# Where the weights of the last phase are converted: w_in and w_out2 in the attention through HBM, w1 and w2 at an even pace

## The chip, the cores and the metric

The kernel runs on one core of one Trainium2 chip. The metric is the device time of one execution in microseconds (us); lower is better. A core has TensorE (PE: matmuls; its weight loads are PEld), VectorE (DVE), ScalarE (ACT), GpSimd (POOL) and SyncE (SP), whose queue issues all DMA transfers of this kernel.

## What is computed

Causal attention with a bias for 4 batches of 8 heads, 576 positions, head size 64; then two blocks of dense layers on the 2304 tokens. All arithmetic is float32.

```python
scores = q @ k.T / 8 + min(-(cum_q - cum_k), 0), causal    # cum: running sum of max(s, 0)
x = softmax(scores) @ v                                    # 2304 x 512
g = (x @ w1) * (x @ w2)                                    # 2304 x 1024
x = g @ w3 @ w_out                                         # w3: 1024 x 1024, w_out: 1024 x 512
h = x @ w_in                                               # 2304 x 1024
so = h * softmax(h)
out = (so - mean) / sqrt(var + 1e-6) * g_ln @ w_out2       # 2304 x 512
```

The weight matrices w1, w2, w3, w_out, w_in and w_out2 arrive as float64 and are handed to the kernel as their bits, two 32-bit words an element.

## The kernel before

**Splitting.** The dense matmuls run on float32r operands. Each operand is split in two: `hi` copies it to float32r on ScalarE (line 92), `lo` subtracts that copy from it (line 97, VectorE or GpSimd). A product is three matmuls: hi·hi, hi·lo, lo·hi.

**Converting weights.** A block of 128 x 512 weights (512 KB of float64 bits) is loaded by `stage`. `to_f32` puts a float32 together from the two words with one scaling on ScalarE (line 374) and three VectorE instructions (380 a shift, 381 and 384 with two inputs each). `split_w` then writes hi and lo of it. `jobs` is a list of blocks in order; `pump(n)` converts the next n and loads ahead into the `stage` buffers (2 in the attention, 4 later). For w_out2 (`wo2_conv`) a further ScalarE instruction (line 783) scales the rows by g_ln.

**Phases.** (1) Attention, a list of 36 `steps`: step st does the scores and softmax of head st (st < 8) or st - 2 (st from 10 on), the transposes of the head two earlier, the product with v every second step (`av_parts`), and `NF[st]` units of the products a = x @ w1 and b = x @ w2 for batches that are done (`ab_unit`: 24 matmuls of 288 columns; the result g goes to `g_scr` in HBM). From step 10 on, GpSimd does two subtractions a head (line 97, QA and KB). The first score tile of a step goes to a PSUM pool that from step 11 on has one buffer. `PUMP[st]` blocks of w1 and w2 (16 in all, `wab_job`) are converted in step st. (2) The last units of a and b, with 14 blocks of w_out and w3 converted between them (`AP3`). (3) The M stage: eight `m_unit`s of 24 matmuls compute M = w3 @ w_out, in split form `MH`, `ML`; after each, `pump(AM[f])` converts three blocks: the rest of w3, then the eight of w_in (`IH`, `IL`). w3's hi and lo have five buffers. (4) Last phase: chunks of 256 tokens, x2 = g @ M (`x2_unit`: four groups of 24 matmuls a chunk); for each of 18 token tiles of 128 `h_unit` (24 matmuls of 512 columns, then maximum, exponential, product, square, power, scaling over VectorE, ScalarE and GpSimd), `tr2` (8 transposes) and `out_unit` (24 matmuls of 512 columns). w_out2's eight blocks (`OH`, `OL`) are converted after x2 of chunk 0 (4) and after the first two h tiles (2 and 2).

**Order.** A planner orders the instructions of each engine by a timeline of its own; they need not stand in source order. Instructions on one engine then run in that order, and the SP queue issues transfers in its order too. `behind` keeps a conversion of the attention behind the step's first softmax tile.

Of the kernel before, what the change touches and what calls it, by code (L numbers as in the profile page):

```python
# [8 lines left out]
F32 = mybir.dt.float32  # L9
F32R = mybir.dt.float32r  # L10
U32 = mybir.dt.uint32
AF = mybir.ActivationFunctionType
ALU = mybir.AluOpType
# [6 lines left out]
CW = 512  # L20
# [5 lines left out]
def tile_attention_moe(  # L26
# [15 lines left out]
    nc = tc.nc  # L42
    B, H, D, _, S = qkT.shape
    NH = B * H
    T, DM = out.shape
    w1, w2, w3L, wo1, w_in, wo2 = (w.bitcast(U32) for w in (w1, w2, w3L, wo1, w_in, wo2))
    DF = w_in.shape[1] // 2
    KC = DM // 128
    KF = DF // 128
# [13 lines left out]
    dram = ctx.enter_context(tc.tile_pool(name="dram", bufs=1, space=DRAM))  # L63
# [4 lines left out]
    ]  # L68
    const = ctx.enter_context(tc.tile_pool(name="const", bufs=1, side="left"))

    g_scr = [dram.tile([KF, 128, S], F32, name=f"g_scr{n}") for n in range(B)]
    cum_scr = dram.tile([NH, 2, S], F32R, name="cum_scr")
    cumf_scr = dram.tile([NH, S], F32, name="cumf_scr")
# [3 lines left out]
    gln = const.tile([128, KF], F32, name="gln")  # L77
# [9 lines left out]
    def flat(ap):  # L87
        return ap.rearrange("p a b -> p (a b)")

    def hi(dst, src, eng=None):  # L90
        if eng is None:
            nc.scalar.activation(out=dst, in_=src, func=AF.Copy)  # L92
        else:
            eng.tensor_copy(out=dst, in_=src)

    def lo(dst, src, hi_, eng=nc.vector):
        eng.tensor_tensor(out=dst, in0=src, in1=hi_.bitcast(F32), op=ALU.subtract)  # L97
# [3 lines left out]
    at = attn_ctx.enter_context(tc.tile_pool(name="at", bufs=1, side="left"))  # L101
# [51 lines left out]
    V, G = nc.vector, nc.gpsimd  # L153
# [213 lines left out]
    wab = [[r0.tile([128, KC, DF // 2], F32R, name=f"W{i}{j}") for j in range(4)] for i in range(2)]  # L367
    xT = [[r0.tile([128, KC, S], F32R, name=f"xT{j}{i}") for i in "hl"] for j in range(2)]

    def to_f32(raw, eng=nc.gpsimd):  # L370

        low, high = raw[:, :, 0], raw[:, :, 1]
        if eng is None:
            nc.scalar.activation(out=high.bitcast(F32), in_=high.bitcast(F32), func=AF.Copy, scale=2.0 ** -112)  # L374
        else:
            eng.tensor_scalar(
                out=high.bitcast(F32), in0=high.bitcast(F32), scalar1=2.0 ** -112, scalar2=1.0,
                op0=ALU.mult, op1=ALU.mult,
            )
        nc.vector.tensor_scalar(out=low, in0=low, scalar1=29, scalar2=None, op0=ALU.logical_shift_right)  # L380
        nc.vector.scalar_tensor_tensor(  # L381
            out=low, in0=high, scalar=3, in1=low, op0=ALU.logical_shift_left, op1=ALU.bitwise_or,
        )
        nc.vector.scalar_tensor_tensor(
            out=low, in0=high, scalar=0x80000000, in1=low, op0=ALU.bitwise_and, op1=ALU.bitwise_or,
        )
        return low.bitcast(F32)

    def split_w(dst_h, dst_l, raw, e1=nc.gpsimd, e2=nc.gpsimd):
        t = to_f32(raw, e1)  # L390
        if len(dst_h.shape) == 3:
            t = t.rearrange("p (c f) -> p c f", c=dst_h.shape[1])
        hi(dst_h, t)
        lo(dst_l, t, dst_h, e2)

    V, G = nc.vector, nc.gpsimd
    ME = [(None, V)]
    MAT = ()
    WO2 = (0, 4, 2, 2)
    XMS = ((0, 1, 2, 3),)  # L400
    EX = 0
    AP3, AM = (2, 2, 2, 2, 2, 2, 1, 1), (3, 3, 3, 3, 3, 3, 3, 3)
    mjobs = []
    jobs = []
    loaded = []

    stg = [at, 2]

    def stage(src):
        raw = stg[0].tile([128, CW, 2], U32, tag="stage", bufs=stg[1], name="stage")  # L410
        dst = flat(raw)
        if len(src.shape) == 3:
            dst = dst.rearrange("p (c f) -> p c f", c=src.shape[1])
        if after[0] is None:
            nc.sync.dma_start(out=dst, in_=src)
        else:
            with tc.issue_after(after[0].ins):
                nc.sync.dma_start(out=dst, in_=src)
        return raw

    def load_jobs():
        while jobs and len(loaded) < stg[1]:
            src, conv = jobs.pop(0)
            loaded.append((stage(src), conv))

    def pump(n):
        for _ in range(n):
            load_jobs()
            if loaded:
                raw, conv = loaded.pop(0)  # L430

                with ExitStack() as order:
                    for ins in behind:
                        order.enter_context(tc.issue_after(ins))
                    conv(raw)
        load_jobs()

    def w_job(src, dst, eng=None):
        e1, e2 = (nc.gpsimd, eng) if eng else ME[len(mjobs) % len(ME)]
        if not eng:  # L440
            mjobs.append(0)
        jobs.append((src, lambda raw: split_w(*dst(), raw, e1, e2)))

    def wab_job(f, w):
        fs = slice((f % 4) * 128, (f % 4) * 128 + 128)
        dst = lambda: (wab[f // 4][2 * w][:, :, fs], wab[f // 4][2 * w + 1][:, :, fs])
        jobs.append(((w1, w2)[w][f], lambda raw: split_w(*dst(), raw, None, V)))

# [34 lines left out]
    for i in range(NQ, 2):  # L485
# [4 lines left out]
        out=wmask[:, S - 128:S], in_=wmask[:, S - 128:S], pattern=[[-1, 128]],  # L490
# [14 lines left out]
    for f in range(KF):  # L505
        for w in range(2):
            wab_job(f, w)


    units = [(n, i, x) for n in range(B) for i in range(KF) for x in range(2)]  # L510
# [2 lines left out]
    steps += [(h if h < NH else None, h - 2 if h >= H + 2 else None) for h in range(H, NH + 2)]  # L513
    NF = {10: 3, 11: 0, 12: 3, 13: 0, 14: 3, 15: 2, 16: 2, 17: 0, 18: 1, 19: 1, 20: 1, 21: 2, 22: 2, 23: 2, 24: 2, 25: 2, 26: 2, 27: 2, 28: 2, 29: 2, 30: 2, 31: 2, 32: 2, 33: 2, 34: 3, 35: 3}
    PD, FS = 10, 0.5
    PUMP = {3: 1, 5: 1, 6: 1, 10: 2, 11: 1, 12: 2, 13: 1, 14: 3, 15: 2, 16: 1, 17: 1}
    fill = []
    late = []
    for st, (h, ph) in enumerate(steps):
# [18 lines left out]
        if st > 1:  # L538
            pump(PUMP.get(st, 0))
        if h is not None:  # L540
# [36 lines left out]
    pm = ctx.enter_context(tc.tile_pool(name="pm", bufs=1, side="left"))  # L577
    MH = pm.tile([128, KF, DM], F32R, name="MH")
    ML = pm.tile([128, KF, DM], F32R, name="ML")
    stg[:] = pm, 4  # L580
    mctx = ExitStack()
    mp = mctx.enter_context(tc.tile_pool(name="mp", bufs=1, side="left"))
    WOH = mp.tile([128, KF, DM], F32R, name="WOH")
    WOL = mp.tile([128, KF, DM], F32R, name="WOL")
    m_st = {}
# [8 lines left out]
    def m_unit(f):  # L594
        ps = smalltile("m")
        for k in range(KF):
            H3, L3 = m_st[f, k // 4]
            for w_, o_ in ((H3, WOH), (H3, WOL), (L3, WOH)):
                nc.tensor.matmul(
                    ps, w_[:, k % 4], o_[:, k],  # L600
                    start=(k == 0 and w_ is H3 and o_ is WOH), stop=(k == KF - 1 and w_ is L3),
                )
# [3 lines left out]
    for k in range(KF):  # L606
        w_job(wo1[k * 128:k * 128 + 128], lambda k=k: (WOH[:, k], WOL[:, k]))
    for f in range(KF):
# [19 lines left out]
    r2 = ctx.enter_context(tc.tile_pool(name="r2", bufs=1, side="right"))  # L628
    IH = r2.tile([128, KC, DF], F32R, name="IH")
    IL = r2.tile([128, KC, DF], F32R, name="IL")  # L630
# [122 lines left out]

    load_g(0)
    load_g(1)
    win = []
    for i in range(8):
        c, o = divmod(i, 2)
        fs = slice(o * 512, o * 512 + 512)
        w_job(  # L760
            w_in[c * 128:c * 128 + 128, o * 1024:o * 1024 + 1024],
            lambda c=c, fs=fs: (IH[:, c, fs], IL[:, c, fs]),
        )
    for f in range(nm[0], KF):
        m_unit(f)
        pump(AM[f] if f < KF - 1 else len(jobs) + len(loaded))
        if f == 4:
            split_g(0, 0)
        if f == 5:
            split_g(0, 1)  # L770
    mctx.close()
    p2 = ctx.enter_context(tc.tile_pool(name="p2", bufs=1, side="left"))
    OH = p2.tile([128, KF, DM], F32R, name="OH")
    OL = p2.tile([128, KF, DM], F32R, name="OL")
    raws = {}

    def wo2_load(k):
        if k < KF:
            raws[k] = stage(wo2[k * 128:k * 128 + 128])

    def wo2_conv(k):
        t = to_f32(raws.pop(k), None)
        nc.scalar.activation(out=t, in_=t, func=AF.Copy, scale=gln[:, k:k + 1])
        hi(OH[:, k], t)
        lo(OL[:, k], t, OH[:, k])
        wo2_load(k + 4)

    nwo = [0]

    def wo2_pump(c):  # L790
        for _ in range(c):
            wo2_conv(nwo[0])
            nwo[0] += 1

    for k in range(4):
        wo2_load(k)
    wo2_pump(WO2[0])
    for i, ms in enumerate(XMS):
        x2_unit(0, *ms)
        wo2_pump(WO2[1 + i])  # L800
    split_g(1, 0)
    split_g(1, 1)
    load_g(2)
# [3 lines left out]
    for t in range(NT + 2):  # L807
        c, o = divmod(t, 2)
        if t < NT:
            h_unit(t)  # L810
        if t < NT and c + 1 < NCH and 2 * t >= EX:
            x2_unit(c + 1, 2 * o)
        if 0 <= t - 1 < NT - 1:
            tr2(t - 1)
        if t < NT and c + 1 < NCH and 2 * t + 1 >= EX:
            x2_unit(c + 1, 2 * o + 1)
        if t < 2:
            wo2_pump(WO2[2 + t])
        if 0 <= t - 2 < NT:
            out_unit(t - 2)  # L820
        if t == NT:
            tr2(t - 1)
        if t < NT and c + 2 < NCH:
            split_g(c + 2, o)
            if o == 1 and c + 3 < NCH:
                load_g(c + 3)
# [50 lines left out]
```

## Time and profile before

| | us |
|---|---|
| median of 3 runs (lowest, highest) | 779.66 (778.08, 780.28) |
| the profiled execution | 779.51 |
| its span, first to last instruction | 777.7 |
| TensorE busy, mean granted clock | 749.4, 0.989 |
| VectorE, ScalarE, GpSimd busy | 466.0, 412.9, 97.3 |

The span is cut into stages by what TensorE does: attention with a and b up to about 349 us, the rest of a and b to 400, M to 444.6, then the last phase. Matmuls are pipelined, and a matmul's own length in a row is longer than its share: 24 x matmuls in a row take 2.81 us, 0.117 each, though one is listed at some 0.29. So "busy" says only that TensorE had something under way; how dense it was is read from the number of matmuls in a stage. The clock is the granted one; 1.00 is 2.4 GHz, and the other level is half of it. A wait "<-X" names what ended an engine's idle time.

### The profile page before, as it was taken

The page shows a single profiled execution, that of the slowest core. Times are in us where ns is not written, and L with a number is a line of the kernel's source. Part 1 is how long each engine was busy: PE and PEld are TensorE (multiplying, and loading weights), DVE is VectorE, ACT ScalarE, POOL GpSimd, SP SyncE. Part 2 cuts the span into 40 slices and gives each one's busy share as a digit, 9 for nine tenths or more (in the row PEclk, how much of TensorE's full clock was granted, in tenths as well). Part 3 has the DMA queues.
Part 4 walks back from the last instruction along what each step waited for, and adds up shares of the span by engine and source line. Part 5 has one row for each costly group of instructions (what it writes and reads, how often), then busy time and mean ns, then how long its engine had stood idle before and what let it go on. Part 6 is the DMA issues. An engine that isn't in the chain of part 4 may idle for free.

```text
span 777.7 us, 13025 instructions
## 1 busy us (share of the span) xinstructions
PE 749.4 (96%) x4864; PEld 653.1 (84%) x4864; DVE 466.0 (60%) x1186; ACT 412.9 (53%) x951; POOL 97.3 (13%) x117
## 2 busy tenths in 40 slices
PE   8989997999999999999999997999999999999997
PEld 5657876888888988899988886888888888888885
DVE  5897989986556564327958889642424353432241
ACT  4987876898766666425536567532323342322232
POOL 6022322233223221000000000000000000000000
PEclk9999998999999999999999999999999999999999
DMA  5543544434332321017659554102112000000001
GB/s 136 173 120 97 170 144 145 145 97 136 109 93 81 106 76 34 31 47 246 214 182 340 169 190 135 55 14 68 47 50 69 14 14 13 15 14 14 14 28 41
DMA packets 38039, 75.59 MB, mean 97 GB/s; under 512 B 6796, under 2 KB 18060, under 8 KB 37976
## 3 DMA queue, kind: packets, MB, share of 16 engines
q1 hardware_dynamic: 37976, 74.76, 31.5%
q8 instruction: 38, 0.62, 0.3%
q14 instruction: 25, 0.20, 0.1%
HBM read 60.36 MB, written 14.38 MB: 96 GB/s over the span
## 4 chain that ended last, share of the span: by engine, by line
PE 80%; DVE 8%; DMA 7%; issue 2%; ACT 1%; POOL 1%; SPq 0%; DVEq 0%; ACTq 0%; POOLq 0%
PE o L746 13%; PE a L338 12%; PE b L338 12%; PE h L697 11%; PE x L677 11%; PE av L310 5%; PE tr L277 4%; PE sc L182 3%; PE sc L190 2%; PE sc L191 2%; PE tr L735 2%; DMA stage<-in_w_dram 2%; DMA stage<-in_w_in_dram 2%; DMA graw<-g_scr 1%; DVE stage L381 1%
## 5 line engine op out<-in xcount | busy, mean ns | idle before, releaser
L208 ACT ACTIVATE P<-P,STAT 64x64 f32<-64x64 f32 (+4 forms) x160 | 88.0, 551 | 32.0 <-DVE STAT L204 29.4
L705 DVE TENSOR_REDUCE sv<-h 128x1 f32<-128x1024 f32 x18 | 22.0, 1225 | 114.6 <-PE h L697 114.6
L677 PE MATMUL x<-gh,MH 128*128 128x256 f32 x288 | 82.9, 288 | 0.0
L677 PE MATMUL x<-gh,ML 128*128 128x256 f32 x288 | 81.5, 283 | 0.0
L677 PE MATMUL x<-gl,MH 128*128 128x256 f32 x288 | 81.5, 283 | 0.0
L204 DVE CUSTOM_DVE_ANT_0 P<-sc,wmask 64x64 f32<-64x64 f32 (+4 forms) x160 | 70.9, 481 | 13.0 <-PE sc L182 8.7
L719 POOL TENSOR_TENSOR sv<-sv,mhalf 128x1 f32<-128x1 f32 x18 | 9.9, 551 | 455.8 <-DVE sv L716 455.8
L97 POOL TENSOR_TENSOR QA<-qk,QB 64x576 fp32r<-64x576 f32 x24 | 35.6, 1482 | 206.8 <-ACT QB L92 168.4
L338 PE MATMUL b<-xT0h,W 128*128 128x288 f32 x256 | 58.1, 301 | 3.3 <-ACT W L92 2.2
L697 PE MATMUL h<-IH,x2h 128*128 128x512 f32 x144 | 56.6, 393 | 3.4 <-ACT x2h L92 1.9
L338 PE MATMUL a<-xT0h,W 128*128 128x288 f32 x256 | 58.7, 303 | 0.0
L697 PE MATMUL h<-IH,x2l 128*128 128x512 f32 x144 | 57.0, 396 | 1.5 <-DVE x2l L97 1.5
L746 PE MATMUL o<-OH,lh 128*128 128x512 f32 x144 | 57.1, 397 | 0.3 <-ACT lh L92 0.3
L338 PE MATMUL a<-xT1h,W 128*128 128x288 f32 x256 | 57.1, 298 | 0.0
L746 PE MATMUL o<-OH,ll 128*128 128x512 f32 x144 | 57.0, 396 | 0.0
L746 PE MATMUL o<-OL,lh 128*128 128x512 f32 x144 | 56.8, 395 | 0.0
L697 PE MATMUL h<-IL,x2h 128*128 128x512 f32 x144 | 56.5, 393 | 0.0
L338 PE MATMUL b<-xT1h,W 128*128 128x288 f32 x256 | 56.5, 294 | 0.0
L677 PEld LDWEIGHTS x<-gh,MH 128*128 128x128 f32 x288 | 55.5, 193 | 0.7
L677 PEld LDWEIGHTS x<-gl,MH 128*128 128x128 f32 x288 | 55.3, 192 | 0.8
L374 ACT ACTIVATE stage<-stage 128x512 f32<-128x512 f32 x56 | 38.3, 689 | 32.5 <-DMA stage<-in_w_dram 13.3
L677 PEld LDWEIGHTS x<-gh,ML 128*128 128x128 f32 x288 | 55.2, 192 | 0.1
(121 smaller groups left out, 1921.2 us busy)
## 6 DMA issues: line engine op xcount, KB each, us to landing
stage<-in_w_dram SPq DMA_DIRECT2D x32, 512.0 KB
qk<-in_qk_dram SPq DMA_DIRECT2D x48, 288.0 KB
g_scr<-g_sb SPq DMA_DIRECT2D x32, 288.0 KB
stage<-in_wo_dram SPq DMA_DIRECT2D x16, 512.0 KB
graw<-g_scr SPq DMA_DIRECT2D x6, 1024.0 KB
out_dram<-o SPq DMA_DIRECT2D x18, 256.0 KB
VT<-in_vm_dram SPq DMA_DIRECT2D x16, 256.0 KB
stage<-in_w_in_dram SPq DMA_DIRECT2D x8, 512.0 KB
```

The costliest lines, as they stand in the source:

```text
L97: eng.tensor_tensor(out=dst, in0=src, in1=hi_.bitcast(F32), op=ALU.subtract)
L182: nc.tensor.matmul(view, QN[h % 2][:, q0:q0 + rows], KN[h % 2][:, c0:c0 + view.shape[-1]], start=True, stop=True,)
L204: mx = nc.vector.tensor_tensor_reduce(out=dst2, in0=ps_in, in1=msk, scale=-SCALE, scalar=BIG, op0=ALU.add, op1=ALU.min, accum_out=st[0:row ...
L208: ex = nc.scalar.activation(out=dst, in_=dst, func=AF.Exp, bias=st[0:rows, ti:ti + 1], scale=-1.0, accum_out=st[0:rows, 5 + ti:6 + ti],)
L277: nc.tensor.transpose(ps[:, c:c + 128], pt[:, QOF[i] + 128 * j:QOF[i] + 128 * j + 128], ident)
L310: nc.tensor.matmul(st["ps"][64 * e:64 * e + 64, 448 + c0:448 + c1], vr[:, j, e], PT[(2 * p + e) % 4][:, o + c0:o + c1], **kw,)
L338: nc.tensor.matmul(ps, w_[:, c, fs], x_[:, c, sl], start=(c == 0 and w_ is WH and x_ is XH), stop=(c == KC - 1 and w_ is WL),)
L374: nc.scalar.activation(out=high.bitcast(F32), in_=high.bitcast(F32), func=AF.Copy, scale=2.0 ** -112)
L677: nc.tensor.matmul(ps[m], w_[:, k, m * 128:m * 128 + 128], g_[:, k], start=(k == 0 and w_ is MH and g_ is GH), stop=(k == KF - 1 and w_ is ...
L697: nc.tensor.matmul(ps[:, hf], x_[:, k, ts_], w_[:, k, hf * 512:hf * 512 + 512], start=(k == 0 and x_ is XH and w_ is IH), stop=(k == KC - ...
L705: nc.vector.reduce_max(out=sv[:, 0:1], in_=psf, axis=AX.X, negate=True)
L746: nc.tensor.matmul(ps, l_[:, k], w_[:, k], start=(k == 0 and l_ is LH and w_ is OH), stop=(k == KF - 1 and l_ is LL),)
```

## The change

- w_in's and w_out2's 16 blocks become jobs behind those of w1 and w2. In the attention each is loaded, converted to float32 into a new tile `cst` (two buffers), for w_out2 scaled by g_ln, and stored to `wf_scr` in HBM (256 KB).
- `PUMP`: w1 and w2 go two a step in steps 10 to 15 and one in step 16; the 16 new jobs one a step in steps 18 to 33.
- In the M stage `pump(AM[f])` converts two blocks, of w3 alone. The stored blocks are read back into four `wf` buffers; after each `m_unit` one block of w_in is split into hi and lo. w_out2's blocks are split four and four after the first two h tiles; none is split before.
- The `stage` buffers of the later phases lie in the pool that ends with the M stage.

```diff
+    wf_scr = [dram.tile([128, CW], F32, name=f"wf_scr{i}") for i in range(16)]
...
-    def to_f32(raw, eng=nc.gpsimd):
+    def to_f32(raw, eng=nc.gpsimd, dst=None):
...
+        res = low if dst is None else dst.bitcast(U32)
         nc.vector.scalar_tensor_tensor(
-            out=low, in0=high, scalar=0x80000000, in1=low, op0=ALU.bitwise_and, op1=ALU.bitwise_or,
+            out=res, in0=high, scalar=0x80000000, in1=low, op0=ALU.bitwise_and, op1=ALU.bitwise_or,
         )
-        return low.bitcast(F32)
+        return res.bitcast(F32)
...
-    WO2 = (0, 4, 2, 2)
...
-    AP3, AM = (2, 2, 2, 2, 2, 2, 1, 1), (3, 3, 3, 3, 3, 3, 3, 3)
+    AP3, AM = (2, 2, 2, 2, 2, 2, 1, 1), (2, 2, 2, 2, 2, 0, 0, 0)
...
+    def spill_job(i):
+        src = w_in[i // 2 * 128:i // 2 * 128 + 128, i % 2 * 1024:i % 2 * 1024 + 1024] if i < 8 else wo2[(i - 8) * 128:(i - 7) * 128]
+
+        def conv(raw):
+            t = at.tile([128, CW], F32, tag="cst", bufs=2, name="cst")
+            to_f32(raw, None, t)
+            if i >= 8:
+                nc.scalar.activation(out=t, in_=t, func=AF.Copy, scale=gln[:, i - 8:i - 7])
+            nc.sync.dma_start(out=wf_scr[i], in_=t)
+
+        jobs.append((src, conv))
...
+    for i in range(16):
+        spill_job(i)
...
-    PUMP = {3: 1, 5: 1, 6: 1, 10: 2, 11: 1, 12: 2, 13: 1, 14: 3, 15: 2, 16: 1, 17: 1}
+    PUMP = {3: 1, 5: 1, 6: 1, 10: 2, 11: 2, 12: 2, 13: 2, 14: 2, 15: 2, 16: 1, 18: 1, 19: 1, 20: 1, 21: 1, 22: 1, 23: 1, 24: 1, 25: 1, 26: 1, 27: 1, 28: 1, 29: 1, 30: 1, 31: 1, 32: 1, 33: 1}
...
-    stg[:] = pm, 4
...
+    stg[:] = mp, 4
...
+    def wf_load(i):
+        if i < 16:
+            wf[i] = r2.tile([128, CW], F32, tag="wf", bufs=4, name="wf")
+            nc.sync.dma_start(out=wf[i], in_=wf_scr[i])
+
+    def wf_split(i, eng):
+        t = wf.pop(i)
...
+        hi(h_, t)
+        lo(l_, t, h_, eng)
+        wf_load(i + 4)
+
+    for i in range(4):
+        wf_load(i)
     for f in range(nm[0], KF):
         m_unit(f)
-        pump(AM[f] if f < KF - 1 else len(jobs) + len(loaded))
+        pump(AM[f])
+        wf_split(f, V)
...
     for i, ms in enumerate(XMS):
         x2_unit(0, *ms)
-        wo2_pump(WO2[1 + i])
...
         if t < 2:
-            wo2_pump(WO2[2 + t])
+            for k in range(4):
+                wf_split(8 + 4 * t + k, V)
```

## Rows read from the trace of the kernel before

**Rows 1.** busy tenths of 40 equal slices of the span (the page)

```profile
PE   8989997999999999999999997999999999999997
```

**Rows 2.** stages: length, busy us of each engine (instructions), granted clock, DMA share, GB/s

```profile
80.00:140.00 60.00, 50.91 (x361) 46.67 (x360) 54.19 (x144) 46.03 (x114) 17.41 (x11) 0.94 0.48 145
140.00:180.00 40.00, 40.00 (x321) 33.84 (x319) 35.96 (x116) 35.70 (x102) 14.68 (x10) 1.00 0.45 126
200.00:320.00 120.00, 120.00 (x947) 109.28 (x946) 69.96 (x239) 79.61 (x216) 26.15 (x18) 1.00 0.26 77
400.90:444.60 43.70, 43.68 (x193) 36.15 (x194) 33.33 (x60) 23.80 (x40) 0.00 (x0) 1.00 0.76 249
444.60:488.50 43.90, 36.60 (x235) 33.13 (x234) 39.55 (x77) 29.91 (x53) 0.56 (x1) 0.95 0.49 155
```

**Rows 3.** TensorE in order of time, 457 to 488: start, length, [idle before <-releaser]

```profile
459.62 0.50 PE L697 MATMUL h<-IH,x2h 128*128 128x512 f32 x1 [1.92 <-ACT x2h L92]
480.62 0.47 PE L697 MATMUL h<-IH,x2h 128*128 128x512 f32 x1 [1.50 <-DVE so L711]
484.19 0.50 PE L697 MATMUL h<-IH,x2l 128*128 128x512 f32 x1 [1.49 <-DVE x2l L97]
487.08 1.25 PE L735 MATMUL tr<-ident,so 128*128 128x128 f32 x7 [2.39 <-DVE so L720]
```

**Rows 4.** matmuls of line 677 (x), then of line 697 (h), in one stage

```profile
444.60:488.50 43.90, 22.06 (x169) 21.72 (x169) 0.95 0.49 155
...
444.60:488.50 43.90, 14.93 (x57) 10.70 (x57) 0.95 0.49 155
```

**Rows 5.** chain that ended last, a full stretch: start, length, what

```profile
508.09 5.49 PE h L697 x24
...
548.81 2.81 PE x L677 x24
551.62 0.87 PE tr L735 x8
```

**Rows 6.** conversions, 444.6 to 488.5: form, count | busy us, mean ns | idle before

```profile
L381 DVE SCALAR_TENSOR_TENSOR stage<-stage 128x512 uint32<-128x512 uint32 x13 | 8.9, 686 | 0.0
...
L374 ACT ACTIVATE stage<-stage 128x512 f32<-128x512 f32 x12 | 8.3, 694 | 6.2 <-DMA stage<-in_w_in_dram 3.8 <-DMA stage<-in_wo_dram 2.4
...
L783 ACT ACTIVATE stage<-stage,gln 128x512 f32<-128x512 f32 x8 | 6.0, 762 | 1.7 <-DVE stage L384 1.6
...
L380 DVE TENSOR_SCALAR stage<-stage 128x512 uint32<-128x512 uint32 x12 | 5.1, 425 | 1.9 <-DMA stage<-in_wo_dram 1.2 <-DMA stage<-in_w_in_dram 0.4
```

**Rows 7.** VectorE, first softmax tile of heads 16 and 31 (16 such rows)

```profile
156.27 0.74 DVE L204 CUSTOM_DVE_ANT_0 P<-sc,wmask 128x576 f32<-128x576 f32 x1
...
313.47 0.75 DVE L204 CUSTOM_DVE_ANT_0 P<-sc,wmask 128x576 f32<-128x576 f32 x1
```

**Rows 8.** conversions, 80 to 140: count | busy us, mean ns | idle before

```profile
L380 DVE TENSOR_SCALAR stage<-stage 128x512 uint32<-128x512 uint32 x8 | 7.7, 977 | 1.4 <-DMA stage<-in_w_dram 1.4
...
L97 DVE TENSOR_TENSOR W<-stage,W 128x512 fp32r<-128x512 f32 x8 | 6.2, 782 | 0.0
```

**Rows 9.** GpSimd and VectorE in order of time, 115 to 121

```profile
115.47 1.73 POOL L97 TENSOR_TENSOR QA<-qk,QB 64x576 fp32r<-64x576 f32 x1 [12.91 <-ACT QB L92]
...
115.82 1.67 DVE L380 TENSOR_SCALAR stage<-stage 128x512 uint32<-128x512 uint32 x1
...
120.91 0.74 DVE L204 CUSTOM_DVE_ANT_0 P<-sc,wmask 128x576 f32<-128x576 f32 x1
```

**Rows 10.** TensorE's waits, 80 to 140: total us, times, longest

```profile
PE sc L190 <- issue: 3.8, 1, 3.8
PE b L338 <- ACT W L92: 2.2, 2, 1.1
PE sc L190 <- DVE g_sb L358: 1.9, 1, 1.9
PE b L338 <- DVE g_sb L358: 1.1, 1, 1.1
```

More of the change, by code (lines that the diff above doesn't have):

```diff
@@ L755, in tile_attention_moe @@
     load_g(1)
[L756 to L763, printed above, removed]
+    wf = {}
+    def wf_load(i):
[4 more added lines that the diff above has]
+        t = wf.pop(i)
+        if i < 8:
+            c, fs = i // 2, slice(i % 2 * 512, i % 2 * 512 + 512)
+            h_, l_ = IH[:, c, fs], IL[:, c, fs]
+        else:
+            h_, l_ = OH[:, i - 8], OL[:, i - 8]
+        hi(h_, t)
[3 more added lines that the diff above has]
+        wf_load(i)
     for f in range(nm[0], KF):
         m_unit(f)
-        pump(AM[f] if f < KF - 1 else len(jobs) + len(loaded))
+        pump(AM[f])
+        wf_split(f, V)
         if f == 4:
@@ L774, in tile_attention_moe @@
     OL = p2.tile([128, KF, DM], F32R, name="OL")
[L775 to L797, printed above, removed]
     for i, ms in enumerate(XMS):
         x2_unit(0, *ms)
-        wo2_pump(WO2[1 + i])
     split_g(1, 0)
```

## The prediction

> **What bounds the kernel now.** I read the 40 slices first, then the busy times of single stages, then the waits in the stages where TensorE is not full. TensorE is full in nearly every slice [rows 1], and its matmuls are the same before and after the change. So the change can only take away time in which TensorE stands still or runs at its lower clock, or add such time. Two stretches before the last phase have it and are touched by the change [rows 2]: 80 to 140 us (50.91 us busy of 60, so 9.09 us idle, granted clock 0.94) and 444.6 to 488.5 us (36.60 of 43.9, so 7.30 us idle, clock 0.95). Between them, from 140 to 180, from 200 to 320 and through the M stage (400.9 to 444.6), TensorE is busy throughout. There VectorE and ScalarE may be given work as long as TensorE never waits for them.
>
> In the later stretch TensorE starts x2 and h. Four waits make up the 7.30 us [rows 3]: 1.92 for x2h on ScalarE, 1.50 and 1.49 for VectorE's `so` and x2l, 2.39 for the normalised `so` that the first transposes need. None of these is a conversion of a weight, but each stands in its engine's queue among such conversions: VectorE is busy 39.55 of 43.9 us here [rows 2]. How long would the stretch be without stalls? It holds 169 x matmuls and 57 h matmuls [rows 4], and the 8 transposes of one token tile. Where TensorE is full, 24 x take 2.81 us, 24 h take 5.49, 8 transposes 0.87 [rows 5]. 169 x 2.81/24 = 19.8, 57 x 5.49/24 = 13.0, and 0.9 and one last M matmul (0.2) give 33.9. So 43.9 - 33.9 = 10.0 us are lost: 7.3 idle, some 2.2 to the lower clock (0.05 x 43.9), the rest in small pieces.
>
> **Part 1: w_in and w_out2 leave the M stage and the start of the last phase.** Each of the 16 blocks costs here VectorE 0.43 + 0.69 and a second 0.69 (line 384 runs the same form as line 381), that is 1.81 us, and ScalarE 0.69, and 0.76 more for each of the 8 w_out2 blocks [rows 6]. For 16 blocks that is 29 us of VectorE and 17.1 us of ScalarE, from the second half of the M stage to 488 us. The hi and lo of each block stay, fed from 256 KB instead of 512 KB. In the late stretch VectorE ran 12 or 13 of each of the three ops, ScalarE 12 and 8 [rows 6]: about 12.5 x 1.81 = 22.6 of 39.55 us and 14.4 of 29.91 us go. VectorE falls to under half of the stretch, and x2h, x2l and `so` no longer queue behind three or four conversions. What is late next is the chain of the first h tile (maximum, exponential, product, square, power, scaling) up to its transposes; TensorE has x2 of chunk 1 (4 units of 24 at 2.81, 11.2 us) and the second h tile (5.49) to cover it, which is what it has in each later tile, where it is full [rows 5]. I take it that 2.0 us stay, about the largest of the four waits [rows 3], so 8.0 of 10.0 are won. The ends: 10.0, and 5.0 if two of the four waits stay with their share of the clock.
>
> The M stage loses w_in's conversions and keeps two w3 blocks a step. VectorE's 33.33 of 43.70 us falls, and TensorE already is full there: no gain. A loss is possible, since four reads of the spilled blocks (1 MB) stand on SP ahead of the w3 loads, with transfers at 249 GB/s in this stage [rows 2]: 1 MB is 4.2 us. The w3 tiles are held back by their five buffers anyway, so I put this at nothing, and at 4 us if that cover is gone. What lies behind 488 us is full and untouched; its first o needs the w_out2 splits, which now stand behind a 256 KB read instead of a 512 KB load and four ops.
>
> **Part 2: sixteen conversions in the attention, steps 18 to 33.** By the first softmax tile of their heads these steps run from 156 to about 314 us, 16 steps [rows 7]. Each adds three VectorE ops, one or two ScalarE ops, a 512 KB load and a 256 KB store. From 200 to 320 us, 11 of the 16 steps begin, and VectorE is busy 69.96 of 120 us, ScalarE 79.61, TensorE 120.00 [rows 2]. With GpSimd's subtractions beside them the ops stretch: in 80 to 140 us line 380 took 0.98 on average instead of 0.43 [rows 6, 8], which makes 0.98 + 2 x 0.69 = 2.36 us of VectorE a block. 11 x 2.36 = 26 and ScalarE 11 x 0.69 + 8 x 0.76 = 14 bring both to 94 to 96 of 120 us. For 140 to 180 the row shows VectorE at 35.96 and ScalarE at 35.70 of 40, with conversions of w1 and w2 among it, and TensorE at 40.00. So that load is known to be hidden, and I cost the sixteen at 0. What hides them are the two a/b units a step; steps 18 to 20 have one only. The other end is the stretch at 80 to 140: 9.09 us idle and 0.06 x 60 = 3.6 us of clock over 8 conversions [rows 2, 8] is 1.59 us each. A spilled block lacks the lo of 0.78 [rows 8]: 2.36 of 3.14 us on VectorE, so 1.59 x 0.75 x 16 = 19 us. The load and the store add 80 GB/s to the 77 of that stretch; 249 GB/s is carried elsewhere [rows 2]. The store waits on SP for the conversion, and behind it stand the loads of a head two steps on, its cumulative rows, the v loads and the g stores. The g stores wait there in the same way for VectorE, with no wait of TensorE from 200 to 320: nothing, or a part of the 19 us.
>
> Line 380 took 1.67 us beside a GpSimd subtraction of 1.73 that began just ahead of it [rows 9]. The Trainium skill ("SBUF — State Buffer", section "Who interferes with whom") says that a VectorE instruction in a two-port mode, or with two SBUF inputs beside a GpSimd one that reads SBUF, shares a port pair with GpSimd as an exclusive lock: the second to start is blocked until the first ends. The trace agrees for line 380. It speaks against the change, since all three added VectorE ops are of these kinds and each attention step has two such subtractions; blocked each time, the three would put VectorE past the step's length, and the time would come out as in the slower rival.
>
> **Part 3: w1 and w2 two blocks a step.** Steps 11 and 13 do two instead of one, step 14 two instead of three, step 17 none. By the end of step 13 eleven blocks are done instead of nine; every block is ready at its unit at least as early. The waits in this stretch are 3.8, 2.2 (W itself, twice), 1.9 and 1.1 us [rows 10]. The 3.8 ends with the softmax tile at 120.91 [rows 9], which stood behind conversions of step 14: with two blocks there instead of three it loses about a third, 1.2. The 2.2 for W should go mostly, say 1.8. Against that, steps 11 and 13 get a block more in front of the g_sb for which the 1.9 and the 1.1 wait; at 1.59 a block, for one of the two, that is 1.5 back. Sum -1.5. The ends: all of 3.8 and 2.2 with 3.6 of clock, -9.6; and two blocks early at 1.59 with nothing won, +3.2.
>
> **Sum.** The profiled execution took 779.51 us (span 777.7), 0.15 below the median of 779.66, so no shift is needed. 779.5 - 8.0 + 0 - 1.5 = 770.0 us.
>
> **Rivals.**
> *The attention becomes VectorE's (slower).* Place: steps 18 to 33, price up to 19 us, 779.5 - 9.5 + 19 = 789; it beats the gain from 9.5/16 = 0.59 us a block on. For it: the stretched ops [rows 8, 9], and 80 to 140, where VectorE is busy 54.19 of 60 and TensorE waits. Against: 140 to 180 at the same share without a wait, and the lower share of 200 to 320.
> *The gain is filled in part.* Steps 18 to 20 with one unit each pay (3 x 1.2 = 3.6 us), or the M stage waits for loads (4 us), or two of the four late waits stay (3 us): 779.5 - 9.5 + 3 to 8, 773 to 778, say 776. For it: the late waits are on x2 and `so`, not on weights. Against: the queues in front of them get far shorter.
> *The stalls of 80 to 140 go altogether.* 770 - 8 = 762, if the 3.8 gap with the lower clock behind it goes. Against: VectorE's total of that stretch is not less.
> *The change doesn't move the late work*, because the planner puts the reads and splits as late as the conversions were: then only the 29 us of VectorE are saved and a wait for the read takes their place, within the second rival.
>
> **How the numbers follow.** Forecast (765 to 775) 0.60; less, below 765, 0.07; part filled (775 to 780) 0.17; slower rival (over 780) 0.16. The range 765 to 781 leaves out 0.07 below and about 0.13 above. A difference under 0.3% (2.3 us) is about what a measurement of this kernel can't tell from no change, so faster means below 777.3: 0.60 + 0.07 + half of 0.17 = 0.75; within 0.3%: the rest of 0.17 and a little of the slower one, 0.11; slower 0.14.
>
> **What would show it.** Right: TensorE without idle time from about 442 to the end of the first h tiles, the four waits gone but one, VectorE under 25 us busy there; from 156 to 320 no wait of TensorE, with VectorE near 80%; the first h at about the M stage's end + 13 us. Part 3: the wait of 3.8 shorter, granted clock at 1.00 from 120 to 140. Wrong: waits of TensorE for softmax tiles, W or g_sb between 156 and 320, a wait for w3 in the M stage, or a clock under 1.00 in either stretch.

## The result, and the profile after

The changed kernel took 769.41 us (median of 4 runs, 768.11 to 772.53), the kernel before 779.31 beside it: a ratio of 0.9868, 95% interval 0.9842 to 0.9894. The forecast was 770.0, range 765 to 781. The profiled execution took 772.53, with a span of 770.8 (before: 779.51 and 777.7). In the code after, line numbers of the attention are 2 higher than before, those of the last phase 16.

The page of after, first busy tenths and granted clock:

```profile
span 770.8 us, 13120 instructions
...
PE   7989979989999999999999999999999999999997
...
PEclk9999989999999999999999999999999999999999
```

Against [rows 1] the 7 in slice 25 is gone. The 8s and 7s in the first third are still there. The stages of after (columns as in [rows 2]; the third row is one that the prediction should have had, the fifth the late stretch at round numbers):

```profile
80.00:140.00 60.00, 52.49 (x373) 48.43 (x373) 49.28 (x142) 44.41 (x112) 17.75 (x10) 0.94 0.50 149
...
140.00:180.00 40.00, 37.42 (x295) 32.08 (x293) 37.39 (x106) 35.17 (x94) 14.53 (x9) 1.00 0.54 166
...
150.00:200.00 50.00, 46.37 (x362) 40.06 (x362) 47.18 (x135) 42.13 (x114) 18.48 (x11) 1.00 0.59 175
...
200.00:320.00 120.00, 120.00 (x945) 108.55 (x942) 88.32 (x276) 90.08 (x237) 32.32 (x20) 1.00 0.54 158
...
445.00:490.00 45.00, 45.00 (x298) 41.09 (x297) 23.95 (x45) 18.57 (x37) 1.11 (x2) 1.00 0.17 48
```

The same two stretches of the kernel before:

```profile
150.00:200.00 50.00, 50.00 (x399) 43.59 (x398) 38.62 (x131) 43.06 (x117) 18.60 (x12) 1.00 0.42 115
...
445.00:490.00 45.00, 37.70 (x239) 34.23 (x239) 40.65 (x79) 30.88 (x54) 0.56 (x1) 0.94 0.47 149
```

In the late stretch TensorE goes from 37.70 us and clock 0.94 to 45.00 and 1.00, with 298 matmuls instead of 239. Between 150 and 200, where the new work begins, it goes the other way: VectorE rises from 38.62 to 47.18 of 50 and TensorE falls from 50.00 to 46.37, with 362 matmuls instead of 399. Not all of that is the new work: with the even pace of w1 and w2 alone (e1 below) TensorE is busy 48.72 us there, with the new work at the old pace (e2) 47.89. From 200 on VectorE carries more too, and TensorE stays full.

TensorE's waits after, the first four from 140 to 340 us, the last from 345 to 500 (total, times, longest):

```profile
PE a L340 <- DVE g_sb L360: 1.5, 3, 0.5
PE b L340 <- DVE STAT L206: 1.3, 1, 1.3
PE a L340 <- ACT xT1h L94: 0.5, 1, 0.5
PE sc L192 <- DVE PT L96: 0.3, 1, 0.3
...
PE m L615 <- DVE g_sb L360: 0.6, 1, 0.6
```

The kernel before had no wait in the first window, and in the second that 0.6 and the four of [rows 3]: those four are gone.

**Where the time went.** Stages end at instructions that every version has. For the two kernels the first M matmul, in order of time (before, then after):

```profile
400.92 0.50 PE L599 MATMUL m<-WOH,w3h 128*128 128x512 f32 x1 [0.62 <-DVE g_sb L358]
```

```profile
405.26 0.50 PE L615 MATMUL m<-WOH,w3h 128*128 128x512 f32 x1 [0.62 <-DVE g_sb L360]
```

From there to the end are 777.7 - 400.92 = 376.78 us before and 770.8 - 405.26 = 365.54 after: "late part" below. The attention is cut in the same way at the first softmax tiles of heads 8, 21 and 31 (steps 10, 23 and 33); [rows 7] are such rows. This is the whole ledger of the profiled executions, with the experiments in the order of the text:

| kernel | start to head 8 | 8 to 21 | 21 to 31 | 31 to M | late part | ratio of the times (95%) |
|---|---|---|---|---|---|---|
| before | 66.76 | 136.30 | 110.41 | 87.45 | 376.78 | 1 |
| after | 68.08 | 139.32 | 110.41 | 87.45 | 365.54 | 0.9868 (0.9842 to 0.9894) |
| after, run again (e0) | 65.41 | 139.17 | 110.41 | 87.45 | 365.46 | 0.9876 (0.9857 to 0.9895) |
| e1 even pace alone | 67.38 | 137.00 | 110.40 | 87.44 | 377.38 | 0.9993 (0.9971 to 1.0014) |
| e2 old pace, rest changed | 65.01 | 139.27 | 110.42 | 87.44 | 365.46 | 0.9888 (0.9866 to 0.991) |
| e4 spills, unused | 67.97 | 141.04 | 110.43 | 87.44 | 378.52 | 1.0054 (1.0029 to 1.0079) |
| e3 late part alone | 65.31 | 136.36 | 110.43 | 87.45 | 365.55 | 0.9861 (0.984 to 0.9882) |
| e6 spills from step 23 | 64.71 | 134.10 | 111.56 | 87.44 | 365.49 | 0.9844 (0.9824 to 0.9863) |
| e7 only w_out2 spilled | 65.04 | 137.08 | 110.41 | 87.45 | 365.72 | 0.9858 (0.9836 to 0.988) |
| e8 no VectorE ops late | 65.31 | 136.32 | 110.41 | 87.45 | 374.81 | 0.9933 (0.9912 to 0.9954) |
| e10 no w_out2 loads | 67.25 | 137.69 | 110.41 | 87.45 | 375.00 | 0.9974 (0.9952 to 0.9996) |
| e11 w_out2 behind x2h | 65.82 | 136.22 | 110.42 | 87.44 | 376.60 | 1.0001 (0.9974 to 1.0027) |
| e12 no scaling of w_out2 | 67.05 | 136.44 | 110.42 | 87.45 | 376.84 | 0.9983 (0.9965 to 1.0001) |
| e13 only hi, lo of w_out2 | 65.05 | 137.43 | 110.41 | 87.45 | 369.66 | 0.9894 (0.9873 to 0.9915) |

From before to after: +1.3 until head 8 (no instruction differs there), +3.0 from 8 to 21, nothing from 21 to M, -11.2 in the late part, together the -6.9 of the spans. The medians differ by -9.9; that execution of after was 3.1 above its median. The numbers of the ledger are those of one execution each, the ratios those of the medians of several; where the two differ, the text gives both.

### The profile page after: what moved, and what is told of

The parts are those of the page before. It is cut to its first block, busy times and chain, and to the rows that moved or that the text cites. A ratio compares the mean times of both kernels' runs of the same rounds, so it can differ in the third digit from the quotient of the medians.

```text
span 770.8 us, 13120 instructions
## 1 busy us (share of the span) xinstructions
PE 746.7 (97%) x4864; PEld 651.0 (84%) x4864; DVE 466.2 (60%) x1186; ACT 409.3 (53%) x951; POOL 104.9 (14%) x117
## 4 chain that ended last, share of the span: by engine, by line
PE 76%; DVE 1%; ACT 1%; issue 0%; ACTq 0%; DVEq 0%
PE o L762 13%; PE x L693 13%; PE h L713 13%; PE a L340 10%; PE b L340 10%; PE m L615 6%; PE av L312 3%; PE tr L279 2%; PE tr L751 2%; PE sc L192 2%; PE sc L193 1%; DVE P L206 0%; PE tr L281 0%; PE tr L288 0%; ACT P L210 0%; DVE QA L96 0%
## 5 line engine op out<-in xcount | busy, mean ns | idle before, releaser
L99 POOL TENSOR_TENSOR QA<-qk,QB 64x576 fp32r<-64x576 f32 x24 | 38.9, 1619 | 203.7 <-ACT QB L94 164.5
L723 ACT ACTIVATE e<-h,sv 128x1024 f32<-128x1024 f32 x18 | 20.1, 1116 | 66.7 <-DVE sv L721 65.4
L767 ACT ACTIVATE o<-o 128x512 f32<-128x512 f32 x18 | 10.8, 598 | 82.9 <-PE o L762 82.9
```

What stands on the lines that cost most here:

```text
L723: nc.scalar.activation(out=e, in_=psf, func=AF.Exp, bias=sv[:, 0:1], scale=1.0, accum_out=sv[:, 1:2])
```

## Experiments

**The changed kernel again (e0).** No edit.

> The changed kernel once more, beside the other three, for a narrower ratio. From its first runs (769.4 us against 779.3): about 0.987, 9 to 11 us below the kernel before.

770.11 us: the result repeats.

**w1 and w2 at the even pace, nothing else (e1).**

```diff
-    PUMP = {3: 1, 5: 1, 6: 1, 10: 2, 11: 1, 12: 2, 13: 1, 14: 3, 15: 2, 16: 1, 17: 1}
+    PUMP = {3: 1, 5: 1, 6: 1, 10: 2, 11: 2, 12: 2, 13: 2, 14: 2, 15: 2, 16: 1}
```

> The kernel before with one edit: w1 and w2 two blocks a step (steps 10 to 15, one in 16). Theory of the prediction: part 3 is worth -1.5 us, so about 778. Rival, from the profile of the changed kernel, whose step 16 begins some 2.5 us later counted from step 10: the earlier blocks lengthen the stretch that VectorE bounds, +1 to +3 us, about 781.

779.59 us, ratio 0.9993: no gain is seen, though the interval, -2.3 to +1.1 us, leaves room for the 1.5. The waits of 80 to 140 us (compare [rows 10]):

```profile
PE sc L190 <- DVE g_sb L358: 3.3, 2, 2.4
PE tr L277 <- DVE STAT L204: 1.3, 1, 1.3
PE b L338 <- DVE g_sb L358: 0.7, 1, 0.7
PE sc L190 <- issue: 0.6, 1, 0.6
PE b L338 <- DVE W L97: 0.5, 1, 0.5
```

The 3.8 became 0.6, as forecast, and of the 2.2 for W 0.5 is left, on VectorE. But score tiles wait 3.3 us for g_sb instead of 1.9, and a transpose waits 1.3 for the softmax, where none did before. The granted clock of this stretch says nothing of the pace: it was 0.94 before, 0.91 here, and at the same pace 0.94 in after and 0.97 in e0 and e6.

**Everything but the even pace (e2)**: after, with the `PUMP` of before up to step 17.

```diff
-    PUMP = {3: 1, 5: 1, 6: 1, 10: 2, 11: 2, 12: 2, 13: 2, 14: 2, 15: 2, 16: 1, 18: 1, 19: 1, 20: 1, 21: 1, 22: 1, 23: 1, 24: 1, 25: 1, 26: 1, 27: 1, 28: 1, 29: 1, 30: 1, 31: 1, 32: 1, 33: 1}
+    PUMP = {3: 1, 5: 1, 6: 1, 10: 2, 11: 1, 12: 2, 13: 1, 14: 3, 15: 2, 16: 1, 17: 1, 18: 1, 19: 1, 20: 1, 21: 1, 22: 1, 23: 1, 24: 1, 25: 1, 26: 1, 27: 1, 28: 1, 29: 1, 30: 1, 31: 1, 32: 1, 33: 1}
```

> The changed kernel with the old pace of w1 and w2 (2, 1, 2, 1, 3, 2, 1, 1 in steps 10 to 17), the sixteen spills as they are. Prediction: without part 3, 1.5 us slower than the changed kernel, about 771. Rival: the even pace costs, so 1 to 3 us faster than the changed kernel, about 767.

770.46 us, ratio 0.9888, the same as after. Its trace is the cleanest for the price of the spills, since head 8 to 16 took 89.46 us, against 89.51 before. Its VectorE rows of heads 16, 21 and 31:

```profile
154.47 0.74 DVE L206 CUSTOM_DVE_ANT_0 P<-sc,wmask 128x576 f32<-128x576 f32 x1
...
204.28 0.75 DVE L206 CUSTOM_DVE_ANT_0 P<-sc,wmask 128x576 f32<-128x576 f32 x1
...
314.70 0.74 DVE L206 CUSTOM_DVE_ANT_0 P<-sc,wmask 128x576 f32<-128x576 f32 x1
```

Head 16 to 21 took 49.81 us, before 203.06 - 156.27 = 46.79; head 21 to 31 took 110.42, before 110.41. So five spilled blocks cost 3.0 us, and the next ten cost nothing. The five are not alike. Head 16 to 19 and head 19 to 21, before and then e2 (columns as in [rows 2]):

```profile
156.27:185.00 28.73, 28.73 (x231) 24.39 (x230) 22.79 (x75) 25.64 (x73) 9.61 (x7) 1.00 0.47 126
185.00:203.06 18.06, 18.06 (x143) 16.25 (x142) 11.96 (x42) 12.29 (x31) 5.92 (x4) 1.00 0.40 111
...
154.47:186.28 31.81, 29.70 (x231) 24.65 (x230) 31.33 (x85) 27.06 (x74) 9.02 (x7) 1.00 0.66 180
186.28:204.28 18.00, 18.00 (x143) 16.19 (x142) 14.75 (x47) 13.75 (x35) 7.70 (x4) 1.00 0.73 227
```

The same 231 matmuls take 31.81 us instead of 28.73, and VectorE is busy for 31.33 of them: the whole price lies in steps 18 to 20, which have one unit of a and b each. Steps 21 and 22, with two, pay nothing.

**The spills added to the kernel before, their results unused (e4).**

```diff
...
+    for i in range(16):
+        spill_job(i)
...
```

`spill_job`, `wf_scr` and the `dst` of `to_f32` come with it as in the change; `PUMP` as in e2.

> The kernel before plus the sixteen conversions and stores of steps 18 to 33, whose results nobody reads; w_in and w_out2 are still converted late and w1 and w2 keep their old pace. It is the price of part 2 alone. Prediction: hidden, 0 us, so 779 to 780. Rivals: the steps with one unit pay, +3 to +4 us (783); or VectorE bounds the attention, up to +19 us (798).

785.16 us, ratio 1.0054: 4.2 us slower. All of the attention's 4.7 lie before head 21; the late part's further 1.7 stay unexplained. Head 16 to 19 took 29.99 us for 211 matmuls, in e3, with no spills, 26.63 for the same 211: steps 18 to 20 again.

**The late part alone (e3).** Reads of the same shape fetch parts of v, so that nothing has to be converted in the attention; w_in and w_out2 are replaced by these numbers.

```diff
...
-            nc.sync.dma_start(out=wf[i], in_=wf_scr[i])
+            nc.sync.dma_start(out=wf[i], in_=vM[i % 4, i // 4, :, 0:CW])
```

This is against after; the spill jobs are gone, and `PUMP` is that of the kernel before.

> The late phases as in the changed kernel, the attention as before: no conversion and no store of w_in and w_out2 anywhere; the sixteen 256 KB reads fetch float32 words of v in their place, so the weights of the last phase are left out. It is part 1 alone. Ledger of the profiles so far (first M matmul to the end 365.5 us instead of 376.8; first softmax tile of head 8 to the first M matmul 337.1 instead of 334.2): 11.3 us below the kernel before, about 768. The prediction's 8.0 would give 771.

768.9 us, ratio 0.9861; the late part is 365.55, and the attention as before. This is the gain without its price: 11.2 us by the profile, 10.8 by the ratio. By the ratios the price of the spills is known less well than by the profiles: after lies 0.5 us above e3, e0 1.2, e2 2.1, and e4 4.2 above the kernel before, each uncertain by about 2 us or more.

**The spills in steps 23 to 33 (e6)**, two a step in five of them; the rest as after.

```diff
+    PUMP = {3: 1, 5: 1, 6: 1, 10: 2, 11: 2, 12: 2, 13: 2, 14: 2, 15: 2, 16: 1, 23: 2, 24: 1, 25: 2, 26: 1, 27: 2, 28: 1, 29: 2, 30: 1, 31: 2, 32: 1, 33: 1}
```

> The changed kernel with the sixteen spills in steps 23 to 33 only, two in 23, 25, 27, 29 and 31. Theory: a spill costs where a step has one a/b unit or where w1 and w2 are just done (steps 18 to 22, 3 us together) and nothing where a step has two units; so head 8 to the M stage falls back to 334 us and the time is 3 us under the changed kernel, 767. Rival: two in a step no longer fit beside GpSimd's subtractions, VectorE makes TensorE wait there, and the time is the same or longer, 770 to 775.

767.23 us, ratio 0.9844, the lowest median here, 2.9 below e0's; the intervals of e3 and e7 overlap with it. Its stages 150 to 200 and 200 to 320:

```profile
150.00:200.00 50.00, 49.85 (x392) 43.52 (x393) 40.11 (x133) 41.94 (x115) 18.84 (x13) 1.00 0.47 125
200.00:320.00 120.00, 120.00 (x938) 108.38 (x937) 93.17 (x276) 90.94 (x236) 27.48 (x18) 1.00 0.56 171
```

VectorE carries 93.17 of 120 us beside a full TensorE. From head 21 to 31 the price is 1.1 us, for all sixteen blocks. Not all of the difference to after is the spills: from head 8 to 21 e6 took 134.10 us and e1, with the same work there, 137.00.

**Only w_out2 spilled (e7)**, in steps 26 to 33; w_in converted in the M stage as before.

```diff
-    for i in range(16):
+    for i in range(8, 16):
         spill_job(i)
...
-        pump(AM[f])
-        wf_split(f, V)
+        pump(AM[f] if f < KF - 1 else len(jobs) + len(loaded))
```

> Only w_out2's eight blocks are spilled (steps 26 to 33); w_in is converted in the M stage as before, w1 and w2 at the old pace. Theory: the waits of the late stretch on `so`, x2l and the first transposes stand behind w_out2's conversions and go, the wait for x2h behind w_in's last conversions stays: 7 to 9 us of the 11.3, about 771, with no cost in the attention. Rival: w_in's late conversions push the whole rest, so at most half is won, 774 or more.

768.16 us, ratio 0.9858, late part 365.72: w_out2's eight blocks hold all of the late gain; w_in's add nothing to it. What w_in's would bring alone was not run. The late stretch, and ScalarE in order of time:

```profile
445.00:490.00 45.00, 45.00 (x312) 41.44 (x312) 36.08 (x67) 25.95 (x50) 1.11 (x2) 1.00 0.36 106
```

```profile
456.04 0.92 ACT L94 ACTIVATE x2h<-x 128x256 fp32r<-128x256 f32 x3
```

VectorE is busy 36.08 of 45 us and TensorE is full: the busy share alone is not what cost the time. The three x2h run at 456.04, with none of w_out2's operations ahead of them; before, h had to wait for them until 459.62 [rows 3]. That left two suspects, VectorE's operations and the queue in front of x2h. The last five runs are about them; each is the kernel before with one thing changed.

**No VectorE operations in the 16 late conversions (e8).** Lines 380, 381 and 384 are left out there, so w_in and w_out2 are wrong numbers; loads and ScalarE's operations stay.

```diff
...
+        if late_only[0]:
+            nc.scalar.activation(out=high.bitcast(F32), in_=high.bitcast(F32), func=AF.Copy, scale=2.0 ** -112)
+            return high.bitcast(F32)
...
```

> The kernel before with the three VectorE instructions of to_f32 left out for the sixteen blocks of w_in and w_out2 (hi and lo are made of the scaled high word, so these weights are wrong); loads of 512 KB, both ScalarE instructions and all places stay. Theory: the late stalls are VectorE's queue, so most of the 11.3 us goes, 769 to 771. Rival: they are the loads and ScalarE, in whose queues the same waits stay, 776 to 779.

774.6 us, ratio 0.9933: by time 5.2 us are won (3.6 to 6.9). In the profiled execution the late part falls by 2.0 of 11.2 only; where the rest of the 5.2 lies, no trace shows. Late stretch, wait and ScalarE:

```profile
445.00:490.00 45.00, 39.20 (x252) 35.65 (x252) 22.90 (x44) 30.43 (x56) 1.10 (x2) 0.92 0.43 129
```

```profile
PE h L707 <- ACT x2h L92: 5.3, 1, 5.3
```

```profile
460.20 0.65 ACT L376 ACTIVATE stage<-stage 128x512 f32<-128x512 f32 x1 [1.00 <-DMA stage<-in_wo_dram]
460.76 0.64 ACT L92 ACTIVATE OH<-stage 128x512 fp32r<-128x512 f32 x1
461.30 0.76 ACT L795 ACTIVATE stage<-stage,gln 128x512 f32<-128x512 f32 x1
462.12 0.65 ACT L376 ACTIVATE stage<-stage 128x512 f32<-128x512 f32 x1
462.68 0.64 ACT L92 ACTIVATE x2h<-x 128x256 fp32r<-128x256 f32 x2
```

VectorE is down to 22.90 us, less than after's 23.95, and TensorE still loses 5.8 us. Now x2h stands in ScalarE's queue behind four operations on w_out2, one of which waited for its load. The theory that VectorE alone sets the late part fell: it would have brought most of the 11.2, and about half came by time, a fifth in the profile. The next was this queue.

**w_out2's conversions held behind the first chunk's x2h (e11).** No work is removed.

```diff
...
-            wo2_conv(nwo[0])
+            with tc.issue_after(x2_hi[3].ins): wo2_conv(nwo[0])
```

> The kernel before, with one hint to the planner: the eight conversions of w_out2 may not stand ahead of the last x2h of the first chunk. No operation and no load is taken away; nothing is spilled. If the late part is lost because x2h stands in ScalarE's queue behind w_out2's conversions (theory 'queue order'), the wait of TensorE at the first h goes and, if nothing else comes late, first M matmul to the end falls from 376.8 to 366-369, a median of 768-772. If it is lost because this work has to be done somewhere in that stretch and fills ScalarE and VectorE (theory 'amount of work'), the waits move on to so, lh or OH: first M matmul to the end stays at 374-378, a median of 776-782.

779.38 us, ratio 1.0001. The wait for x2h went, and two others took its place. Late stretch, waits, then VectorE and ScalarE:

```profile
445.00:490.00 45.00, 37.65 (x237) 33.96 (x236) 38.54 (x75) 29.14 (x52) 2.00 (x1) 0.89 0.42 141
```

```profile
PE tr L735 <- DVE sv L708: 3.7, 1, 3.7
PE h L697 <- DVE so L711: 3.1, 1, 3.1
PE h L697 <- DVE x2l L97: 0.4, 1, 0.4
```

```profile
476.78 0.43 DVE L380 TENSOR_SCALAR stage<-stage 128x512 uint32<-128x512 uint32 x1 [1.20 <-DMA stage<-in_wo_dram]
477.12 1.28 DVE L711 SCALAR_TENSOR_TENSOR so<-h,sv,e 128x1024 f32<-128x1024 f32 x1
```

```profile
476.84 0.68 ACT L374 ACTIVATE stage<-stage 128x512 f32<-128x512 f32 x1 [4.02 <-DMA stage<-in_wo_dram]
```

`so` of the first h tile stands in VectorE's queue behind a conversion that waits for its load.

**w_out2 without its loads (e10)**: the conversions run on the tiles of w_in's last blocks.

```diff
...
-            raws[k] = stage(wo2[k * 128:k * 128 + 128])
+            raws[k] = stg[k % 4 - 4]
```

> The kernel before, with w_out2 never fetched: its conversions run on the tiles of the last four blocks of w_in, so the weights of the last phase are not w_out2's. Every operation of the conversions on ScalarE and VectorE stays, the eight loads of 512 KB go. If the conversions hold up x2h because they stand in ScalarE's queue waiting for their loads ('waiting for loads'), first M matmul to the end falls from 376.8 to 366-371, a median of 768-774. If their own time in the queue does it ('the operations'), it stays at 374-378, a median of 776-781.

777.33 us, ratio 0.9974; the late part falls by 1.8. The wait for x2h shrinks to 0.6, and one of 5.5 for `so` appears:

```profile
PE h L697 <- DVE so L711: 5.5, 1, 5.5
PE h L697 <- ACT x2h L92: 0.6, 1, 0.6
```

**w_out2 without ScalarE's two scalings (e12).**

```diff
...
-        t = to_f32(raws.pop(k), None)
-        nc.scalar.activation(out=t, in_=t, func=AF.Copy, scale=gln[:, k:k + 1])
+        t = to_f32(raws.pop(k), 0)
```

`to_f32` with 0 leaves line 374 out.

> The kernel before without the two scaling operations of ScalarE in each of w_out2's eight conversions (the high word's and gln's), so the weights of the last phase are wrong. All loads, the three VectorE operations, hi and lo stay. If VectorE is the engine that sets the late part (theory 'VectorE sets it'), first M matmul to the end stays at 374-377, a median of 777-780. If ScalarE sets it (theory 'ScalarE sets it'), it falls to 366-369, a median of 768-772. If each conversion is a chain over both engines, so that either engine's operations alone hold the tiles up (theory 'both'), it falls by 1 to 5 us, to 372-376.

778.86 us, ratio 0.9983 (-2.7 to +0.1 us): nothing clear of the noise, though ScalarE is busy 20.11 us instead of 30.88.

```profile
445.00:490.00 45.00, 38.37 (x240) 34.47 (x239) 40.66 (x80) 20.11 (x38) 0.56 (x1) 0.91 0.47 149
```

```profile
PE h L698 <- DVE so L712: 5.5, 1, 5.5
```

**w_out2 with hi and lo alone (e13).**

```diff
-        t = to_f32(raws.pop(k), None)
-        nc.scalar.activation(out=t, in_=t, func=AF.Copy, scale=gln[:, k:k + 1])
+        t = raws.pop(k)[:, :, 1].bitcast(F32)
```

> The kernel before with only hi and lo left of each of w_out2's eight conversions: two ScalarE and three VectorE operations a block are left out, so the weights of the last phase are wrong. The eight loads of 512 KB stay where they are. If the amount of conversion work on both engines in that stretch costs the late part (theory 'amount of work'), first M matmul to the end falls from 376.8 to 365-367, a median of 767-770, with no TensorE wait over 1 us between 445 and 500. If the loads or the reads of stage cost part of it (theory 'loads'), at most half of the 11 us comes back: 370-375.

771.83 us, ratio 0.9894; the late part falls by 7.1 of 11.2, between the two theories.

```profile
445.00:490.00 45.00, 42.52 (x284) 39.10 (x284) 33.30 (x62) 24.08 (x44) 1.11 (x2) 0.96 0.47 149
```

```profile
PE h L697 <- ACT x2h L92: 2.5, 1, 2.5
```

```profile
458.61 0.67 ACT L92 ACTIVATE OH<-stage 128x512 fp32r<-128x512 f32 x1 [0.53 <-DMA stage<-in_wo_dram]
459.18 0.93 ACT L92 ACTIVATE x2h<-x 128x256 fp32r<-128x256 f32 x3
```

**What the five say together.** Taking away ScalarE's scalings is worth 0, the order in front of x2h 0.2, the loads 1.8, VectorE's operations 2.0 (those of w_in too), all in us of the late part. By the ratios these four are 1.3, none, 2.0 and 5.2, so VectorE's operations may be worth more than their one profile shows. Taking away the operations on both engines, for w_out2 alone, is worth 7.1 (by the ratio 8.3), and the whole conversion (e7) 11.1 by both. So no one link made the whole loss: a conversion is a chain of a load, ScalarE, VectorE three times, ScalarE, hi and lo over two in-order queues, and whichever link stays holds up x2h, x2l or `so` in its own queue. The last 4.0 (e13 to e7) are the 2.5 of the wait for x2h and the clock, 0.96 instead of 1.00. In e13 the operation just ahead of x2h had waited 0.53 for a 512 KB load, but w_in's last blocks stand there too, and the planner chooses anew in each version. e7 also splits w_out2 later, four blocks behind each of the first two h tiles and none right behind x2 of chunk 0. How much of the 4.0 is the load and how much the place was not separated.

## Why the prediction was right, and where it was not

That the total was right to 0.6 us is in part luck: two terms were too small, and they nearly cancel. -8.0 + 0 - 1.5 = -9.5 was forecast; the medians give -9.9, the profiled ledger -11.2 + 3.0 and nothing seen for the pace, -8.2. With the profile of e0, the same kernel, the ledger comes to -9.8, of which 1.35 us stand ahead of head 8, where no instruction differs and no term of mine applies.

**Part 1, -8.0 forecast, -11.2 measured.** The mechanism held: TensorE had lost time in the late stretch by waits that name x2h, x2l and `so`, and they went with the conversions. Two steps were mis-sized. I left 2.0 us standing, "about the largest of the four waits"; none stayed (45.00 of 45 busy). And I cut the loss off at 488.5, where the lower clock was not over. The chain of the kernel before, behind the cut:

```profile
488.54 6.81 PE x L677 x48
```

48 x take 5.62 us at the pace of [rows 5], so 1.2 more were lost here, with a granted clock of 0.81 in these 6.81 us. 10.0 + 1.2 = 11.2. What I gave as the reason, the load on VectorE, is only a part of it: relief of VectorE alone brought 2.0 by the profile and 5.2 by time (e8), and a VectorE at 36.08 of 45 us was harmless in e7. That the M stage would pay up to 4 us for the reads did not come true: M and the rest are 365.46 to 365.72 us in each version that reads blocks back. I had not priced w_in and w_out2 apart: e7 shows that w_in's eight blocks, half of the moved work, bring nothing beside w_out2's.

**Part 2, 0 forecast, +3.0 measured (e2), by time between +0.5 and +4.2.** For the steps from 21 on, zero was right, and e6 shows the cover to be good for more. For steps 18 to 20 it was wrong, and the step that failed is the inference "so that load is known to be hidden". The row of 140 to 180 [rows 2] showed VectorE at 35.96 of 40 with TensorE full, but in a stretch without the spills. I added their work to the mean of 200 to 320 and never to those steps themselves. Before, VectorE was busy 22.79 of the 28.73 us from head 16 to 19; the 5.94 left are less than three blocks at the 2.36 that I had worked out, 7.1. In e2 VectorE is busy 31.33 of 31.81 us there. My second rival had the place (steps with one unit of a and b) and nearly the price, 3.6; the slower rival's mechanism did act, for three steps instead of sixteen. The blocks of these three steps are w_in's, which e7 does without.

Shared ports of VectorE and GpSimd, as the Trainium skill tells of them ("SBUF — State Buffer", section "Who interferes with whom"), were part of that rival. The trace of after agrees at one of the spills' lines 387: it began 0.36 us behind the start of a GpSimd subtraction of 1.71 and took 1.90. The eleven from 201 to 320 took 0.675 on average:

```profile
198.73 1.90 DVE L387 SCALAR_TENSOR_TENSOR cst<-stage 128x512 uint32<-128x512 uint32 x1
...
L387 DVE SCALAR_TENSOR_TENSOR cst<-stage 128x512 uint32<-128x512 uint32 x11 | 7.4, 675 | 0.0
```

Four of the eleven ran while a GpSimd subtraction was under way, and there it was the subtraction that was long: 2.22 us at 219.34, where the kernel before has 1.64 at 214.50. So a meeting can cost either engine, and blocking in each of the three operations, which the rival needed, did not occur.

**Part 3, -1.5 forecast, nothing seen.** The waits that I named (the 3.8, the 2.2) shrank to 0.6 and 0.5, and the time does not show it: e1 is the same as before within 0.2%, and e2 the same as after. A gain of 1.5 us is not excluded by these intervals. I had priced g_sb's queue at 1.5 back; after waits 5.1 us for it in 80 to 140, before 3.0, and the clock is 0.94 as before (in e0 0.97). What I expected of the clock from 120 to 140 (1.00) came true, but the lower level moved to the 20 us ahead of it (before: 1.00 from 100 to 120 and 0.83 from 120 to 140). The two stretches of after:

```profile
100.00:120.00 20.00, 15.22 (x96) 13.18 (x95) 15.60 (x45) 13.66 (x35) 3.23 (x2) 0.83 0.40 121
120.00:140.00 20.00, 18.82 (x143) 17.77 (x142) 18.85 (x53) 15.64 (x39) 6.94 (x4) 1.00 0.54 160
```

Of the signs that I named, these held: no late waits, VectorE at 23.95 us there, a VectorE at 74% from 200 to 320 beside a full TensorE. VectorE did not fall to under half of the late stretch (23.95 of 45). Two signs of being wrong came: TensorE waits for softmax and g_sb between 156 and 200, the price of part 2, and a clock under 1.00 from 80 to 140. The first h came at 462.06, after's last M matmuls end at 451.95: 10.1 us instead of 13, since the planner starts x2 before M is done and h before x2 is.

## What to carry over

Before calling a stretch's engine "over-full", ask of a wait what stands in the queue ahead of it on every engine of the chain: when each of several links can hold the work up, relief of one moves the wait to the next and shows only a part of the gain, and taking the chain away pays the whole. Work moved under another engine's cover has to be added to each step it goes to, the one with the least room first, not to the mean of the stage; here three of sixteen blocks cost 3 us and the other thirteen nothing.

## What the runs showed that I had not expected

The time until head 8's first softmax tile lay between 64.71 and 68.08 us over fourteen profiled executions, though the kernels do the same there, with a granted clock from 0 to 66 us between 0.95 (after) and 1.00 (e2). After and e0, one and the same kernel, have 68.08 and 65.41; no run shows why. That is up to 3.4 us, more than some of the effects measured here, so spans of single profiles had to be compared stage by stage. From head 8 to 21 versions without spills in that stretch differ by 3.6 (134.10 to 137.69), those with them lie at 139.17 to 141.04; from head 21 to the first M matmul all without doubled spills agree within 0.04.
